# Linear attention and eight routed experts on one core: the overflow spread in two passes, the tails of two experts' q as one block, and the fallback's branch inside the program

## The chip, the cores and the metric

The kernel runs on one core of a Trainium2 chip: TensorE (PE in the tables), VectorE (DVE), ScalarE (ACT), GpSimd (POOL), SyncE (SP) and 16 DMA engines. The metric is the device time of one execution in microseconds, the median of several runs.

## The reference

Attention is linear: q is softmaxed over its 64 head elements, k over the 576 positions of a batch, and each of the 8 heads of a batch has one 64 x 64 matrix kv. Every one of the 4608 tokens (8 batches of 576) then goes to one of eight experts, which is chosen by its id alone; w1 of an expert is 512 x 1024, w2 1024 x 512.

```python
def _attn_ref(q, k, v) -> np.ndarray:
    q_s = q - np.max(q, axis=-1, keepdims=True)
    q_s = np.exp(q_s)
    q_s = q_s / (np.sum(q_s, axis=-1, keepdims=True) + 1e-09)
    ...
    k_s = k_s / (np.sum(k_s, axis=2, keepdims=True) + 1e-09)
    kv = np.einsum('bhsd,bhse->bhde', k_s, v)
    return np.einsum('bhsd,bhde->bhse', q_s, kv).astype(np.float32)
...
    expert_idx = token_ids * np.int64(2654435761) % np.int64(E)
    out = np.zeros((N, D), dtype=np.float32)
    for e in range(E):
        mask = expert_idx == e
        ...
        xe = x[mask]
        h = np.maximum(xe @ w1[e], 0.0)
        out[mask] = h @ w2[e]
```

## The kernel before

**Slots.** Each expert has 640 slots (CAP): 72 for each of the 8 batches (576, MAINC) and 64 for overflow, tokens beyond 72 of one batch and expert. q is gathered by token straight into slot order, five gathers for an expert (four of 128 rows, and a *tail* of 64). Overflow tokens are gathered apart, in batch order, and their X is *spread* to the experts' last 64 slots by matmuls with one-hot matrices.

**Steps.** All work behind the index search is cut into named steps, each a few instructions. The list ORDER, written into the file, is the order in which they are issued; every engine runs its own instructions in that order, and only semaphores tie the engines to each other. SWAP names the evacuations that change between ACT and DVE. A name with `*n` puts n dummy matmuls of 512 columns (line 345) ahead of the step. The names that the text uses:

- K, V: load of a batch's k and v; EK, MK: its exponential and column of ones on ACT; KV: its 20 matmuls; SC: its scaling on DVE (lines 381 to 387), after which kv of the batch can be used.
- G, EQ, SM, ML: gather of a block of q, its exponential, sums over the heads for two or three blocks, scaling; TP, TC: transposition of a block and its evacuation; with an O, the same for overflow.
- CNT, OVA, OHA, FND, FDD: the search for overflow tokens; QS: the one-hots of the spread; ROP, ROD: the row indices of the outputs. CNT also sets a flag that says that some expert has more overflow than its slots hold.
- PP, PC: attention product of blocks of q with the kv of some batches (72 columns for a batch and expert) and its evacuation: this is X, transposed.
- XP, XC: overflow X of two batches, and its copy `xov`; SH, SD: spread of all four, for 128 of the 512 elements, and its evacuation into `XTov`; OV: copy from there into an expert's X.
- W: a half of w1 or w2 of an expert (cast to f16 by the DMA); A: first matmul of an expert (MLP) for a range of slots; R: its relu; B: second matmul of a block of 128 slots; C: its evacuation; S: the scatter of its rows to the output.

**Queues.** k of batches 0 to 2 is loaded by SP; all other loads, gathers and scatters are issued by POOL one after the other, each with a semaphore that it shares with the one eight issues earlier.

**The fallback.** If the flag is set, the scatters write nothing, and `_any_routing` computes everything again in a slower way. Before, the register load of the flag and the branch stand behind all other work (lines 961 to 963); the body is never entered for these inputs.

## Time and profile before

| | |
|---|---|
| median of 3 runs | 224.19 us (224.01 to 224.94) |
| the profiled execution | 224.46 us |
| its span | 222.6 us |
| PE busy | 189.1 us (85%) |
| DVE, ACT, POOL busy | 62%, 52%, 55% |
| DMA queue of POOL | 46.66 MB, 82.0% of the 16 engines' span |

The profile is of one execution. A busy PE is not a PE at its peak: its matmuls overlap, so distances from start to start tell more than durations. "Idle before" names what ended the idle time of an engine. The page's slices are fortieths of the span, 5.57 us each.

### The profile page before, as it was taken

What the parts mean: (1) busy time and instruction counts of PE and PEld (TensorE: products, weight loads), DVE (VectorE), ACT (ScalarE), POOL (GpSimd) and SP (SyncE); (2) the same over time, 40 slices, a digit from 0 to 9 for tenths busy, and PEclk for the clock granted to TensorE, in tenths of its full rate; (3) what the DMA queues carried; (4) which work ended last, traced back from release to release, by engine and by line L of the source; (5) the groups of instructions that cost most, each with busy time, mean ns of one, the idle gap of its engine ahead of it and who ended that gap; (6) DMA issues with size and microseconds to landing.
All of it is one profiled execution on the core that took longest, in us unless ns stands there. A gap on an engine that the chain in (4) does not pass through costs nothing.

```text
span 222.6 us, 3981 instructions
## 1 busy us (share of the span) xinstructions
PE 189.1 (85%) x1533; PEld 124.1 (56%) x1533; DVE 137.8 (62%) x259; ACT 116.6 (52%) x189; POOL 122.9 (55%) x160
## 2 busy tenths in 40 slices
PE   3506165398999999999999999999999999999990
PEld 2507164276567666755776565666665556655540
DVE  6998797668778897697842989675424431022230
ACT  8347555994779877574564655433451224432210
POOL 7675567445378885587785161611543367315661
PEclk9999857559999999999999999999999999999998
DMA  6999999999999999799999968670997999943442
GB/s 209 321 329 389 234 345 329 322 245 296 292 280 274 292 247 267 221 244 233 266 308 216 239 146 155 148 165 3 175 234 167 188 186 195 284 110 135 166 165 85
DMA packets 13543, 50.67 MB, mean 228 GB/s; under 512 B 2650, under 2 KB 2650, under 8 KB 12496
## 3 DMA queue, kind: packets, MB, share of 16 engines
q0 software_dynamic: 12944, 46.66, 82.0%
q1 hardware_dynamic: 576, 3.71, 4.3%
q8 instruction: 13, 0.21, 0.4%
q14 instruction: 10, 0.08, 0.1%
HBM read 63.10 MB, written 10.49 MB: 331 GB/s over the span
## 4 chain that ended last, share of the span: by engine, by line
issue 38%; POOL 21%; PE 20%; DMA 11%; DVE 6%; ACT 2%; POOLq 1%; DVEq 0%
POOL out_dram L550 12%; PE ph L523 7%; DMA kraw<-in_k_dram 4%; PE po L545 4%; DMA out_dram<-ob,sidx 3%; DMA w1r<-in_moe_w_dram 3%; POOL raw L395 3%; PE t L372 2%; POOL w1r L508 2%; PE t L436 2%; PE t L476 2%; POOL w2r L508 2%; DVE A L126 1%; PE t L447 1%; PE t L469 1%
## 5 line engine op out<-in xcount | busy, mean ns | idle before, releaser
L545 PE MATMUL po<-w2r,hT 128*128 128x512 f16 (+2 forms) x328 | 74.8, 374 | 0.0
L523 PE MATMUL ph<-XT,w1r 128*128 128x320 f16 (+2 forms) x512 | 74.6, 297 | 0.0
L536 ACT ACTIVATE hT<-ph 128x640 f16<-128x640 f32 (+3 forms) x58 | 40.5, 703 | 55.3 <-PE ph L523 54.6
L550 POOL DMA_INDIRECT out_dram<-ob,sidx x40 | 42.6, 1065 | 44.7 <-DVE ob L938 29.6
L523 PEld LDWEIGHTS <-w1r 128*128 128x128 f16 x544 | 49.3, 98 | 21.2
L395 POOL DMA_INDIRECT raw<-in_q_dram,gidx x40 | 42.9, 1071 | 20.7 <-issue 4.9
L938 DVE TENSOR_SCALAR ob<-po 128x512 f32<-128x512 f32 x34 | 23.1, 683 | 43.8 <-PE po L545 39.4
L545 PEld LDWEIGHTS <-hT 128*128 128x128 f16 x328 | 30.9, 98 | 30.4
L418 DVE TENSOR_REDUCE rq<-qs 128x16 f32<-128x1024 f16 (+1 forms) x18 | 26.1, 1450 | 3.8 <-ACT qs L406 3.7
L424 DVE TENSOR_TENSOR qs<-qs,rq 128x1024 f16<-128x1024 f16 (+1 forms) x18 | 26.1, 1456 | 0.4
L406 ACT ACTIVATE qs<-raw 128x512 f16<-128x512 f32 (+1 forms) x40 | 23.6, 625 | 0.8 <-DMA raw<-in_q_dram,gidx 0.8
L436 PE MATMUL t<-ident,qs 128*128 128x128 f16 (+1 forms) x176 | 15.8, 226 | 4.8 <-ACT qT L879 2.6
L879 DVE COPY qT<-t 128x512 f16<-128x512 f16 (+3 forms) x18 | 8.5, 478 | 15.6 <-PE t L436 15.3
L508 POOL DMA_DIRECT2D w2r<-in_moe_w_dram x16 | 9.5, 595 | 14.3 <-PE po L545 10.1
L436 PEld LDWEIGHTS <-qs 128*128 128x128 f16 (+1 forms) x176 | 12.0, 103 | 9.1 <-issue 4.3
L372 PE MATMUL t<-v,w1r 128*128 128x129 f16 x64 | 8.0, 293 | 7.5 <-ACT v L360 7.5
L508 POOL DMA_DIRECT2D w1r<-in_moe_w_dram x16 | 9.5, 595 | 5.8 <-PE ph L523 3.7
L372 PEld LDWEIGHTS <-w1r 128*128 128x128 f16 x64 | 6.9, 139 | 7.5 <-issue 7.4
L372 PE MATMUL t<-v,w2r 128*128 128x129 f16 x64 | 5.9, 243 | 5.9 <-DVE rec L381 5.9
L907 DVE CAST XT<-t 128x288 f16<-128x288 f32 (+2 forms) x18 | 7.9, 453 | 4.2 <-PE t L447 3.9
L913 ACT CAST XT<-px 128x864 f16<-128x864 f32 (+1 forms) x7 | 5.6, 811 | 8.6 <-PE px L459 8.6
L879 ACT COPY qT<-t 128x512 f16<-128x512 f16 (+2 forms) x14 | 7.9, 581 | 3.9 <-PE t L436 3.9
(125 smaller groups left out, 187.9 us busy)
## 6 DMA issues: line engine op xcount, KB each, us to landing
w1r<-in_moe_w_dram POOLq DMA_DIRECT2D x16, 512.0 KB, 8.0
w2r<-in_moe_w_dram POOLq DMA_DIRECT2D x16, 512.0 KB, 7.7
kraw<-in_k_dram POOLq DMA_DIRECT2D x3, 1024.0 KB, 9.2
v<-in_v_dram POOLq DMA_DIRECT2D x4, 650.0 KB, 10.2
kraw<-in_k_dram SPq DMA_DIRECT2D x2, 1280.0 KB, 11.2
kraw<-in_k_dram POOLq DMA_DIRECT2D x2, 1280.0 KB
v<-in_v_dram POOLq DMA_DIRECT2D x4, 520.0 KB, 8.5
kraw<-in_k_dram SPq DMA_DIRECT2D x1, 1024.0 KB, 11.3
```

The source lines that it names most:

```text
L372: nc.tensor.matmul(pkv[:, r // 2, r % 2, 0:129], lhsT=k16t[:, f] if last else k16[:, c, f], rhs=v16s[e][:, c * NPAIR + r, 0:129] if last e ...
L395: nc.gpsimd.indirect_dma_start(out=raw[0:w, :], out_offset=None, in_=self.q[:, :], in_offset=bass.IndirectOffsetOnAxis(ap=idx[0:w, i:i + 1 ...
L406: self.nc.scalar.activation(q16[0:w, i].rearrange("p h d -> p (h d)"), raws[i][0:w, :], ACT.Exp)
L418: nc.vector.reduce_sum(rv, qv, axis=AX.X)
L424: nc.vector.tensor_tensor(out=qf, in0=qf, in1=rv.rearrange("p i h -> p (i h)").unsqueeze(2) .to_broadcast([w, (hi - lo) * H_, DH_]), op=AL ...
L436: nc.tensor.transpose(pv[:, r, o:o + w[j]], q16[0:w[j], j, 2 * r:2 * r + 2, :] .rearrange("p h d -> p (h d)"), self.ident[0:w[j], 0:w[j]])
L508: self.nc.gpsimd.dma_start(w[what - 1][:, 2048 * i:2048 * i + 2048], src[e, :, 2048 * i:2048 * i + 2048])
L523: nc.tensor.matmul(p, lhsT=w1r[:, dc, f[i] * 128:(f[i] + 1) * 128], rhs=X[:, dc, :], start=(dc == 0), stop=(dc == DC - 1))
L536: self.nc.scalar.activation(to, fro, ACT.Relu)
L545: nc.tensor.matmul(po[:, 0:d.stop - d.start], lhsT=hT[:, fc, blk * 128:(blk + 1) * 128], rhs=w2r[:, fc, d], start=(fc == 0), stop=(fc == F ...
L550: sc = self.nc.gpsimd.indirect_dma_start(out=self.out[:, :], out_offset=bass.IndirectOffsetOnAxis(ap=self.ix.sidx[:, e, blk:blk + 1], axis=0),
L938: nc.vector.tensor_scalar(out=obs[e, blk][:, d], in0=po[e, blk, x][:, 0:d.stop - d.start], scalar1=1.0 / SX, scalar2=None, op0=ALU.mult)
```

## The change

**Spread in two passes.** SH now multiplies only batches 0 to 3 (the first two `xov`) and SD puts the result into `XTov`. New steps SI and SE do the other half: SE (`join`) adds the bank to what `XTov` holds, in place, on DVE.

**Tails as one block.** Block 4 of an even expert holds its own 64 tail rows and, in partitions 64 to 127, those of the next expert. Odd experts have four blocks. All gathers, exponentials, sums and transposes are of 128 rows, and the transposed tail block is evacuated for both experts at once. Its indices take one matmul more and one DVE operation; the two ACT copies that filled the unused halves go.

**The branch.** A step ANY, behind FDD, loads the flag and jumps over the body, on every engine, while the rest of the program stands behind it. `_any_routing` is rewritten to work with 128 tokens at a time in buffers that the main program has not filled yet; it is never entered here.

**ORDER and SWAP** are other lists. 24 dummy matmuls stand in it (KV2\*9, TPO_1\*7, XP0\*4, PP0_02\*4) where there were 8.

```diff
+        tail = pp[:, NB:NB + E_MOE]
+        nc.tensor.matmul(tail, lhsT=shift[:, 64:192], rhs=g16[:, PLACE[B_ - 1], :], start=True, stop=True)
...
+        V.tensor_scalar(out=gidx[64:128, 0:E_MOE:2, BPE - 1], in0=tail[64:128, 1:E_MOE:2],
+                        scalar1=float(S_ * (B_ - 1) - 1), scalar2=None, op0=ALU.add)
...
-        for i in range(2):
-            nc.scalar.copy(self.q16s[i][64:128, BPE - 1].rearrange("p h d -> p (h d)"),
-                           self.two[64:128, 0:1].to_broadcast([64, D_MOE]))
...
-    def gather(self, idx, widths, lo, hi, into=None):
+    def gather(self, idx, lo, hi, into=None):
         nc = self.nc
         raws = {}
-        for i, w in list(enumerate(widths))[lo:hi]:
+        for i in range(lo, hi):
             raw = into[i] if into else self.qpool.tile([128, D_MOE], F32, tag="qraw", bufs=10)
             nc.gpsimd.indirect_dma_start(
-                out=raw[0:w, :], out_offset=None, in_=self.q[:, :],
-                in_offset=bass.IndirectOffsetOnAxis(ap=idx[0:w, i:i + 1], axis=0),
+                out=raw[:, :], out_offset=None, in_=self.q[:, :],
+                in_offset=bass.IndirectOffsetOnAxis(ap=idx[:, i:i + 1], axis=0),
                 bounds_check=N_TOK - 1, oob_is_err=False)
...
         return pt
 
-    def shared(self, xovs, Qs, r):
+    def shared(self, xovs, Qs, r, ns):
         pr = self.bank("T")
-        for n in range(NBP):
+        for n in ns:
             self.nc.tensor.matmul(pr[:], lhsT=xovs[n][:, r * 128:(r + 1) * 128], rhs=Qs[n],
-                                  start=(n == 0), stop=(n == NBP - 1))
+                                  start=(n == ns[0]), stop=(n == ns[-1]))
         return pr
 
     def spread(self, pr, r):
         put = self.nc.scalar.copy if other(f"SD{r}", r % 2 == 1) else self.nc.vector.tensor_copy
         put(self.XTov[:, :, r, :], pr[:].rearrange("p (e i) -> p e i", e=E_MOE))
+
+    def join(self, pr, r):
+
+        x = self.XTov[:, :, r, :]
+        self.nc.vector.tensor_tensor(out=x, in0=pr[:].rearrange("p (e i) -> p e i", e=E_MOE), in1=x, op=ALU.add)
 
 
 def other(name, put):
...
-def _any_routing(nc, tc, q, k, v, token_ids, w1, w2, out):
+def _any_routing(nc, tc, q, k, v, token_ids, w1, w2, room, ident, w, ps, pool, out):
...
-MK0 EK1 MK1 CNT G0_2 EK0 G0_0 EQ0_2 OVA ZO1 KV1 G0_1 EQ0_0 KV0 EQ0_1 ZO0 OHA FND K3 FDD G0_3 V2 EK2 QS SM0a
...
+ZO0 CNT MK0 OVA G0_2 OHA FND G0_1 G0_0 EK1 V2 ZO1 MK1 EQ0_0 G0_3 EK0 EQ0_2 EQ0_1 K3 EK2 FDD ANY V3 KV1 G0_4
...
-        QW = [128] * (BPE - 1) + [MAINC - 128 * (BPE - 1)]
+
+        def blocks(e):
+            return NBP if e == "O" else BPE - e % 2
         eng = mybir.EngineType
...
+            wts[0] = moe.new_weights(wa)
+
+            def anyway():
+                more = nc.values_load(flag[0:1, 0:1], min_val=0, max_val=1)
+                with tc.If(more > 0, label="any"):
+                    _any_routing(nc, tc, q, k, v, moe_token_ids, moe_w1, moe_w2, (qT, XTs[0], hs[0], at.XTov),
+                                 at.ident, wts[0], ps, fpool, out)
+
+            add("ANY", anyway)
...
+                n = blocks(e)
                 for i in range(n):
                     add(f"G{e}_{i}", gather, e, i, i + 1)
                     add(f"EQ{e}_{i}", lambda e, i: at.expq(qs[e], i, i + 1), e, i)
-                for x, lo, hi in (("a", 0, 2), ("b", 2, 4)) if e == "O" else (("a", 0, 3), ("b", 3, 5)):
...
-                        (A if other(f"TC{e}_{i}", e < 2) else V)(qT[:, :, e % 4, 128 * i:128 * i + sum(QW[i:i + m])], pq[e, i])
-                for i, m in [(i, 1) for i in range(n)] if e == "O" or e < 4 else ((0, 2), (2, 1), (3, 2)):
+                        if i < BPE - 1:
+                            to, fro = qT[:, :, e % 4, 128 * i:128 * (i + m)], pq[e, i]
+                        else:
+                            to, fro = qT[:, :, e % 4:e % 4 + 2, 128 * i:], pq[e, i].rearrange("p r (k t) -> p r k t", k=2)
+                        (A if other(f"TC{e}_{i}", e < 2) else V)(to, fro)
+                for i, m in [(i, 1) for i in range(n)] if e == "O" or e < 4 else ((0, 2), (2, 2), (4, 1))[0:n - 2]:
                     add(f"TP{e}_{i}", lambda e, i, m: pq.update({(e, i): at.turn(qs[e], i, m)}), e, i, m)
                     add(f"TC{e}_{i}", turnc, e, i, m)
             for n in range(NBP):
...
-                add(f"SH{i}", lambda i: pr.update({i: at.shared(xovs, Qs, i)}), i)
+                add(f"SH{i}", lambda i: pr.update({i: at.shared(xovs, Qs, i, (0, 1))}), i)
                 add(f"SD{i}", lambda i: at.spread(pr[i], i), i)
+                add(f"SI{i}", lambda i: pr.update({i: at.shared(xovs, Qs, i, (2, 3))}), i)
+                add(f"SE{i}", lambda i: at.join(pr[i], i), i)
...
-    more = nc.values_load(flag[0:1, 0:1], min_val=0, max_val=1)
-    with tc.If(more > 0, label="any"):
-        _any_routing(nc, tc, q, k, v, moe_token_ids, moe_w1, moe_w2, out)
 
```

On POOL, from the load of k of batch 6 (`kraw_620`, after: `kraw_918`) on, before:

```order
L781 DMA kraw_620<-in_k_dram 128x2560
L785 DMA v_6_625<-in_v_dram 128x2600
L395 DMA raw<-in_q_dram,gidx 128x512
L508 DMA w1r<-in_moe_w_dram 128x2048 x2
L781 DMA kraw_763<-in_k_dram 128x2048
L785 DMA v_7_783<-in_v_dram 128x2080
```

and after:

```order
L785 DMA kraw_918<-in_k_dram 128x2560
L789 DMA v_6_926<-in_v_dram 128x2600
L785 DMA kraw_929<-in_k_dram 128x2048
L789 DMA v_7_933<-in_v_dram 128x2080
L509 DMA w1r<-in_moe_w_dram 128x2048 x2
L396 DMA raw<-in_q_dram,gidx 128x512 x6
```

The two halves of w1 of expert 0 have moved from before k and v of batch 7 to behind them.

On DVE, behind the one-hots of the overflow search (`AO`), before:

```order
L240 TENSOR_TENSOR AO<-rowi,Z 128x2304
L262 COPY ov<-po 64x8 x2
L264 TENSOR_SCALAR of<-ov 128x4
L265 TENSOR_TENSOR of<-ov,obase 128x4
L266 TENSOR_TENSOR oidx<-of 128x4
L268 CAST part<-ov 128x4
L269 CAST part<-obase 128x4
L276 TENSOR_SCALAR Q<-rowi,ov 128x512 x4
L418 TENSOR_REDUCE rq<-qs_109 128x24
```

and after (the body of the branch, which is not entered, stands between the jump and the sums):

```order
L825 MEMSET rawo_292 128x512
L825 MEMSET rawo_293 128x512
L266 COPY ov<-po 64x8 x2
L268 TENSOR_SCALAR of<-ov 128x4
L269 TENSOR_TENSOR of<-ov,obase 128x4
L270 TENSOR_TENSOR oidx<-of 128x4
L272 CAST part<-ov 128x4
L273 CAST part<-obase 128x4
L836 TENSOR_LOAD flag
L837 COMPARE_AND_BRANCH
```

Two memsets and the branch stand in this stretch now; the one-hots `Q` come later.

On PE, the last steps ahead of the first MLP matmul (`ph<-XT`), before: the end of overflow X of batches 4 and 5 (`kvr_106` is batch 5) and a transposition:

```order
L469 LDWEIGHTS qTo_284
L469 MATMUL t<-kvr_106,qTo_284 128x128
L436 LDWEIGHTS qs_109
L436 MATMUL t<-ident,qs_109 128x128
...
L523 LDWEIGHTS w1r
L523 MATMUL ph<-XT_294,w1r 128x432
```

and after: the end of the second spread pass (`xov`, batches 4 to 7), products of expert 1 with batches 6 and 7 (`kvr_107`, `kvr_108`) and with 0 to 3:

```order
L472 LDWEIGHTS xov_1200
L472 MATMUL t<-Q,xov_1200 128x512
...
L443 LDWEIGHTS kvr_107
L443 MATMUL t<-qT,kvr_107 128x72
L443 LDWEIGHTS kvr_108
L443 MATMUL t<-qT,kvr_108 128x72
...
L524 LDWEIGHTS w1r
L524 MATMUL ph<-XT_294,w1r 128x432
```

KV7, the whole first pass of the spread and half of the second, the transposes of expert 1 and most of its products have moved ahead of that matmul.

## Rows read from the trace of the kernel before

**Rows 1.** The page's slices of 5.57 us: TensorE's busy tenths, and its granted clock
```profile
PE   3506165398999999999999999999999999999990
...
PEclk9999857559999999999999999999999999999998
```

**Rows 2.** Timeline of PE: start us, us, engine, line, operation, xcount, idle before
```profile
54.03 0.29 PE L447 MATMUL t<-qT,kvr 128*128 128x72 f16 x4
54.16 0.39 PE L372 MATMUL t<-v,w2r 128*128 128x129 f16 x4
...
56.24 3.08 PE L523 MATMUL ph<-XT,w1r 128*128 128x432 f16 x16
...
60.95 0.39 PE L436 MATMUL t<-ident,qs 128*128 128x128 f16 x4
61.17 0.39 PE L372 MATMUL t<-v,w2r 128*128 128x129 f16 x4
...
62.31 1.62 PE L523 MATMUL ph<-XT,w1r 128*128 128x432 f16 x8
...
63.77 0.61 PE L469 MATMUL t<-kvr,qTo 128*128 128x128 f16 x8
...
64.84 0.44 PE L447 MATMUL t<-qT,kvr 128*128 128x72 f16 x4 [0.33 <-DVE XT L907]
...
65.12 3.62 PE L476 MATMUL t<-Q,xov 128*128 128x512 f16 x16
...
209.54 7.09 PE L545 MATMUL po<-w2r,hT 128*128 128x512 f16 x40
```

**Rows 3.** Timeline of POOL, 49 to 61 us: issues, and the landing waited for
```profile
49.79 1.00 POOL L395 DMA_INDIRECT raw<-in_q_dram,gidx  x1 [1.38 <-DMA v<-in_v_dram]
...
52.62 1.00 POOL L395 DMA_INDIRECT raw<-in_q_dram,gidx  x1 [0.52 <-DMA w1r<-in_moe_w_dram]
...
55.15 0.57 POOL L508 DMA_DIRECT2D w2r<-in_moe_w_dram  x1 [1.53 <-DMA w1r<-in_moe_w_dram]
...
57.56 0.96 POOL L395 DMA_INDIRECT raw<-in_q_dram,gidx  x1 [1.84 <-DMA kraw<-in_k_dram]
...
60.20 1.01 POOL L395 DMA_INDIRECT raw<-in_q_dram,gidx  x1 [1.68 <-DMA v<-in_v_dram]
```

**Rows 4.** Timeline of VectorE (DVE), 24 to 70 us
```profile
24.12 1.14 DVE L276 TENSOR_SCALAR Q<-rowi,ov 128x512 f16<-128x512 f16 x4
...
25.18 1.75 DVE L418 TENSOR_REDUCE rq<-qs 128x24 f32<-128x1536 f16 x1
...
30.15 1.76 DVE L424 TENSOR_TENSOR qs<-qs,rq 128x1536 f16<-128x1536 f16 x1
...
31.82 1.21 DVE L418 TENSOR_REDUCE rq<-qs 128x16 f32<-128x1024 f16 x1
...
33.57 1.22 DVE L424 TENSOR_TENSOR qs<-qs,rq 128x1024 f16<-128x1024 f16 x1
...
39.18 0.16 DVE L381 TENSOR_SCALAR rec<-t 128x4 f32<-128x4 f32 x1
...
40.48 0.29 DVE L879 COPY qT<-t 128x256 f16<-128x256 f16 x1
...
69.08 0.68 DVE L482 CAST XTov<-t 128x512 f16<-128x512 f32 x1
```

**Rows 5.** Lines 961 and 962, the branch: queue, operation, ns, first and last start us
```profile
L961 DVEq TENSOR_LOAD <-flag x1: 541/541/541, 214.9 to 214.9; - x1
...
L962 SPq EVENT_SEMAPHORE  x8: 17/17/17, 14.4 to 18.8; - x8
...
L962 SPq COMPARE_BRANCH  x1: 45/45/45, 14.0 to 14.0; - x1
...
L962 DVEq EVENT_SEMAPHORE  x1: 21/21/21, 216.2 to 216.2; - x1
```

**Rows 6.** Timeline of ACT (ScalarE): a wait at 18 us, a copy of overflow X
```profile
18.18 0.22 ACT L360 COPY v<-two 128x32 f16<-128x32 f16 x1 [2.20 <-DMA v<-in_v_dram]
...
64.42 0.59 ACT L886 CAST xov<-t 128x512 f16<-128x512 f32 x1 [0.64 <-PE t L469]
```

More of the change, by code (lines that the diff above doesn't have):

```diff
@@ L402, in expq @@
     def expq(self, rq16, lo, hi):
-        raws, q16, widths = rq16
+        raws, q16 = rq16
         for i in range(lo, hi):
-            w = widths[i]
-            self.nc.scalar.activation(q16[0:w, i].rearrange("p h d -> p (h d)"), raws[i][0:w, :], ACT.Exp)
+            self.nc.scalar.activation(q16[:, i].rearrange("p h d -> p (h d)"), raws[i][:, :], ACT.Exp)
     def soften(self, rq16, lo, hi):
@@ L429, in turn @@
         nc = self.nc
-        q16, w = rq16[1], rq16[2]
         pq = self.bank("Q")
         pv = pq[:].bitcast(F16).rearrange("p (r t) -> p r t", r=NPAIR)
-        for j in range(i, i + n):
-            o = 128 * (j - i)
+        for j in range(n):
             for r in range(NPAIR):
-                nc.tensor.transpose(pv[:, r, o:o + w[j]], q16[0:w[j], j, 2 * r:2 * r + 2, :]
-                                    .rearrange("p h d -> p (h d)"), self.ident[0:w[j], 0:w[j]])
-        return pv[:, :, 0:sum(w[i:i + n])]
+                nc.tensor.transpose(pv[:, r, 128 * j:128 * j + 128], rq16[1][:, i + j, 2 * r:2 * r + 2, :]
+                                    .rearrange("p h d -> p (h d)"), self.ident[:])
+        return pv[:, :, 0:128 * n]
     def product(self, qT, r, lo, hi, es, q0=0):
@@ L651, in _any_routing @@
                 for dc in range(DC):
                     nc.tensor.transpose(px[:, dc, :], xm[:, dc * 128:(dc + 1) * 128], ident[:])
-                xT = pool.tile([128, DC, 128], F16)
-                nc.scalar.copy(xT[:], px[:])
+                nc.scalar.copy(xT, px)
                 ph = ps.tile([128, 2, 512], F32, tag="S")
@@ L659, in _any_routing @@
                                          start=(dc == 0), stop=(dc == DC - 1))
-                h16 = pool.tile([128, 2, 512], F16)
-                nc.scalar.activation(h16[:], ph[:], ACT.Relu)
-                pt = ps.tile([128, FC, 128], F16, tag="T")
+                nc.scalar.activation(h16, ph[:].rearrange("p i f -> p (i f)"), ACT.Relu)
+                pt = ps.tile([128, 512], F32, tag="Q", name="gq")[:].bitcast(F16).rearrange("p (f t) -> p f t", f=FC)
                 for fc in range(FC):
-                    nc.tensor.transpose(pt[:, fc, :], h16[:, fc // 4, 128 * (fc % 4):128 * (fc % 4) + 128], ident[:])
-                hT = pool.tile([128, FC, 128], F16)
-                nc.scalar.copy(hT[:], pt[:])
-                po = ps.tile([128, D_MOE], F32, tag="O")
+                    nc.tensor.transpose(pt[:, fc, :], h16[:, 128 * fc:128 * fc + 128], ident[:])
+                nc.scalar.copy(hT, pt)
+                po = ps.tile([128, 512], F32, tag="T")
                 for fc in range(FC):
                     nc.tensor.matmul(po[:], lhsT=hT[:, fc, :], rhs=w2r[:, fc, :], start=(fc == 0), stop=(fc == FC - 1))
-                a = acc[:, bass.ds(m, 1), :].rearrange("p o f -> p (o f)")
-                nc.vector.scalar_tensor_tensor(out=a, in0=po[:], scalar=1.0 / SX, in1=a, op0=ALU.mult, op1=ALU.add)
-        nc.sync.dma_start(out.rearrange("(n p c) f -> p n c f", n=NBP, c=C9),
-                            acc[:].rearrange("p (n c) f -> p n c f", c=C9))
+                nc.vector.scalar_tensor_tensor(out=acc, in0=po[:], scalar=1.0 / SX, in1=acc, op0=ALU.mult, op1=ALU.add)
+            nc.sync.dma_start(rows(out)[bass.ds(n, 1), :, bass.ds(c * D_MOE, D_MOE)].rearrange("o p f -> (o p) f"), acc)
 PARTS = ((0, slice(0, 1), ((0, 4), (4, 6), (6, 8))), (1, slice(1, 2), ((0, 4), (4, 8))),
@@ new lines @@
+TPO_3 EK7 SC5 MK7 SH0 SC4 TCO_3 G2_1 PC1_03 KV6 G2_2 TPO_2 SC6 TCO_2 PP0_41 SD3 KV7 SD0 PC0_41 PP0_43 PP0_42
+SC7 XP2 PC0_42 PP0_40 PC0_43 PC0_40 PP1_01 XP3 PC1_01 PP0_61 XC2 G3_0 PP0_62 G3_2 PC0_61 PP1_43 XC3 PC0_62
+W11_1 PP1_40 PC1_43 SI1 PC1_40 SI3 PP1_42 PP1_00 SE1 G3_3 PC1_42 PC1_00 A0_0_2 SI0 EQ3_1 SE3 PP0_63 A0_0_0
+W11_0 PP0_60 G2_3 R0_0_2 SE0 W02_1 SI2 PC0_63 PP1_41 EQ3_0 R0_0_0 W02_0 G5_2 EQ2_1 G4_4 SM3a A0_0_1 R0_0_1
+PC0_60 SE2 A0_0_3 PC1_41 ML3a R0_0_3 A0_576_0 EQ2_2 A0_432_0 A0_432_1 TP3_1 OV1 EQ2_0 R0_432_0 A1_0_0 R0_432_1
@@ L864 @@
             for e in (*range(E_MOE), "O"):
-                n = NBP if e == "O" else BPE
+                n = blocks(e)
                 for i in range(n):
```

269 lines of the change are left out of this document (133 added, 136 removed).

## Prediction

> **What bounds the kernel now.** Read the page's slices first [rows 1]: TensorE (PE) is ragged in the first eleven slices, then at nine tenths or more up to the last; its granted clock is at the lower level (1.2 GHz) in slices 5, 7 and 8 and at 2.4 GHz from slice 9 on. Then the timeline of PE [rows 2]: the first matmul of expert 0's MLP starts at 56.24 us, the last group of matmuls ends at 209.54 + 7.09 = 216.63: 160.4 us in which the slices show no visible hole. The time is therefore one sum: *the moment when the first MLP matmul may start* (call it T), plus the PE work that is still to do then, plus the last scatter and closing barrier. The span is 222.6 us and the profiled execution took 224.46, 0.27 above the median of 224.19; I sum against 224.46 and take the difference over to the median.
>
> What holds T is read from the DMA queue on POOL [rows 3]: POOL's next gather waits again and again for a landing: v of batch 6 by 49.8, the two halves of w1 of expert 0 by 52.6 and 55.15, k of batch 7 by 57.6, v of batch 7 by 60.2. Each is about 1.05 MB read from HBM and each takes 2.4 to 2.8 us: a full pipe in which order is all.
>
> **The change, part by part.**
>
> *The new order at PE.* Before, the first MLP matmul stands behind batches 0 to 6 only; KV7, the spread and expert 1's transposes run after it. Now the first MLP matmul stands behind all of these. What has moved ahead of T, by start-to-start times [rows 2]: KV7, 62.31 - 61.17 = 1.1; the last overflow X, at most 0.6, taken as 0.45; four transposed blocks of expert 1 at 61.17 - 60.95 = 0.22 each, 0.9; eight groups' worth of four 72-column products at 54.16 - 54.03 = 0.13 each, 1.0; 12 of the 16 spread matmuls, 12/16 of 3.62, taken as 2.6 to 2.7. Sum 6.1. The merged tails take another 0.2 off what is left (an estimate: of the transposes behind T, 28 of 64 columns become 12 of 128, these at 0.22/4 = 0.055 each, the short ones at about half). Behind T the old order also waited some 0.65 us around the spread, 0.33 of it in the row at 64.84 and the rest in smaller gaps beside it; that wait would now lie before T. So the new kernel ends when the old one does if T = 56.24 + 6.3 + 0.65 = **63.2 us**; every microsecond of T above or below that is one of the time.
>
> *How early can T be: the loads.* The order list shows w1 of expert 0 ahead of k and v of batch 7 before, and behind them now. V7 moves up by the two halves of w1 (55.15 - 49.79 = 5.4 us), and is pushed back by more q rows ahead of it: nine full gathers of 128 x 512 f32 against four full and two half ones, 1.05 MB, one piece as above, 2.4 us. V7 lands at 60.2 - 5.4 + 2.4 = 57.2, and the second half of w1 at 57.2 + 2 x 2.5 = 62.2. T is not before **62.2**.
>
> *How early: VectorE (DVE).* From its first softmax sum up to the scaling of batch 7, DVE must now do: one three-block sum and scale (1.75 + some 0.6, and 1.76), five two-block sums (33.57 - 31.82 = 1.75), five two-block scales (1.22), eight kv scalings (40.48 - 39.18 = 1.30), the four one-hots of Q (1.14), the four small operations that make row indices (0.9), and nine evacuations of 0.3 to 0.7 (two spread banks like the 0.68 one) [rows 4], 4.3: 4.1 + 8.75 + 6.1 + 10.4 + 1.1 + 0.9 + 4.3 = **35.7 us** without a gap. It can begin at about 24.2: the two memsets ahead of the counts (1 us) only trade places with two behind, so the search for overflow ends 1.4 us earlier than before, at some 22.7, and the branch lies behind it. ACT (ScalarE) needs until 24 for the three exponentials, since its wait for v of batch 1 (18.18, [rows 6]) stays. One gap is certain (the second sum waits for its fifth block of q, which lands near 31: three pieces of 0.4 to 1.05 MB behind k of batch 3, by the same pace): 0.9 us. So batch 7 is scaled at 60.8, and then come the last overflow X 0.45, its copy on ACT 0.59 [rows 6], two of the second-pass spread matmul pairs 0.9 and four hand-offs of 0.15 to 0.25: T = **63.4 to 64.0**. The loads would allow 62.2; DVE is later by 1.2 to 1.8.
>
> *The branch.* It costs each engine a register load and a jump in mid-stream: on DVE 214.9 to 216.2, 1.3 us [rows 5]; the same order on PE, ACT and POOL. On DVE it is covered by the wait for ACT's exponentials; on POOL the queue has several microseconds of transfers outstanding; on ACT it is in front of work that waits for its loads anyway; PE waits there for softmax. Behind the branch on DVE the sum of expert 0 is queued, for which the transposes wait. I take 0, and 1.3 if the covers fail. At the kernel's end its removal is worth nothing: the register load there runs while the last scatter is being issued, and the end waits for that scatter's landing.
>
> *What is off the path.* Four gathers fewer on POOL (1.0 us each, [rows 3]), four exponentials of a half-empty block fewer on ACT, about 4 us of sums and scales less on DVE (four times the difference between a three-block and a two-block sum and scale, 0.6 + 0.5), against four joins of the second pass (one operation over a bank each; the nearest row is the spread's evacuation, 0.68, and I bound a join by half and twice of it). Most of it lies behind T, where PE is the only full engine; the joins of the first two banks stand beside expert 0's first matmuls, and need be done only before the 64-column part. 0 for all of it. The two ACT fills of tails that go stand where ACT next waits for its first data. The extra tail matmul and index operation of expert pairs add 0.2 us ahead of the first gathers; the memset's place covers it. The body of the rewritten branch never runs here.
>
> Sum: T is 63.4 to 64.0 against 63.2, 0.2 to 0.8 us longer; I take 0.6: 225.1 for the profiled run, **224.8** for the median. That is no change that can be measured (0.5% is 1.1 us, about what a measurement can tell).
>
> **The rivals.**
>
> *Slower, by the clock.* In the old run PE was thin between 34 and 44 us and its granted clock was at the lower level up to slice 8 [rows 1]; it rose only near 50 us, when PE had become denser. In the new order PE waits for DVE between KV7 (from 57.5) and T, with some 2 us of work in 5. If the clock falls there, the first matmuls of the MLP run at half speed: the 16 of the first two chunks take 3.08 us at the full one ([rows 2]), so 1.5 to 3 us are lost. For it: the engine was no thinner before its earlier fall. Against: 24 dummy matmuls instead of 8 are put into the waits, though all of them well ahead of KV7. It decides where the clock is low at T: 226.3 to 227.8. Chance 0.2.
>
> *Slower, by front engines that slip.* DVE would be 97% busy for 36 us, in program order. Each wait of DVE for PE's banks adds itself to T. Two more microseconds give 226.8. A dearer branch belongs here: SP jumps at 14.0 us, in a full pipe, and its first semaphore operation follows within half a microsecond [rows 5], so I keep the chance small. But an engine whose next instructions had to be fetched first would stand still, and the fetch would stand behind one to three of the pieces of rows 3 that are in flight, 2.5 to 7.5 us on DVE, which has no slack: 227 to 232. (The Trainium skill, "Runtime: NRT & Kernel Launch", Instruction fetch mechanics, states such a rule: a taken branch whose target is not in the two pages held forces a DMA fetch of that page. By that rule the price above applies where DVE's target lies further on; SP's row shows no such stall, and no run here shows where DVE's target lies.) Chance of a slip 0.17, of the fetch 0.05.
>
> *Faster.* If DVE keeps up and the loads alone bound T (62.2 to 62.5), the time is 223.3 to 223.6. For it: the loads' order is the better one for batch 7. Against: w1 is then needed the moment it lands. More than 0.5% needs T below 62.1, at the bound of the loads, which I know to about 1 us: chance 0.18.
>
> *The halves do not spread.* If both passes ran back to back at the old place the split would only add the joins; the order shows the first pass between batch products, so this is not the case.
>
> **How the numbers follow.** No measurable change 0.40 (own range 223.6 to 225.3); clock 0.2, slip 0.17, fetch 0.05, together slower 0.42; faster 0.18. The range 222.9 to 227.7 leaves out the fetch and about half of the extremes on either side.
>
> **What would show it.** First MLP matmul at 63 to 64 us; V7 landed near 57 and w1 near 62; DVE without a gap from 24 to 60; PE full for 153.4 us (160.4 less 6.3 and 0.65) from T to its last matmul; granted clock at 2.4 GHz when T comes. Wrong would be: T above 65 (slip, or a gap of 3 us behind the branch on DVE or PE), T right but the first 432-column matmuls 364 ns apart (clock), or T near 62 with DVE waiting for loads (faster).

## The result and the profile after

| | before | after |
|---|---|---|
| median of 5 runs each, us | 224.31 (224.01 to 224.94) | 222.05 (221.51 to 222.19) |
| profiled execution | 224.46 | 222.19 |
| first MLP matmul (T) | 56.24 | 62.59 |
| T to the end of the last matmul | 160.4 | 152.5 |
| of it beyond matmuls at their usual distance | 2.0 | 0.3 |
| end of the last matmul to the end of the span | 5.97 | 5.31 |
| outside the span | 1.86 | 1.80 |

The ratio is 0.9888 with an interval of 0.9866 to 0.991: the changed kernel is 1.1% faster. That lies under the predicted range, on the side that was given 0.18. The "usual distance" is from one matmul's start to the next: 0.216 us for 512 columns, 0.182 for 432, 0.136 for 320, 0.056 for 128, 0.029 for 64. Summed over all matmuls from T to the last they make 158.15 us before and 151.93 after.

The slices that answer to [rows 1]. TensorE is still thin in front, but in this execution its granted clock is at 2.4 GHz from 32.1 us to the last matmul. (The nines ahead of that are no sign of the clock: the 129-column products of batch 1, at 27 us, stand 0.11 us apart, those of batch 3, at 35 us, 0.056.)
```profile
PE   3501098669899999999999999999999999999990
...
PEclk9999999999999999999999999999999999999999
```
The timeline of PE that answers to [rows 2]: the second spread pass, the last products ahead of T, T itself, and the last group of matmuls.
```profile
61.47 1.03 PE L472 MATMUL t<-Q,xov 128*128 128x512 f16 x4
...
62.34 0.42 PE L443 MATMUL t<-qT,kvr 128*128 128x72 f16 x8
...
62.59 1.63 PE L524 MATMUL ph<-XT,w1r 128*128 128x432 f16 x8
...
207.99 7.09 PE L546 MATMUL po<-w2r,hT 128*128 128x512 f16 x40
```
The timeline of POOL that answers to [rows 3]. Batch 7 lands before w1 now: v of batch 7 by 57.05 us, the last half of w1 by 62.01.
```profile
52.13 1.00 POOL L396 DMA_INDIRECT raw<-in_q_dram,gidx  x1 [0.52 <-DMA v<-in_v_dram]
54.56 1.00 POOL L396 DMA_INDIRECT raw<-in_q_dram,gidx  x1 [1.43 <-DMA kraw<-in_k_dram]
57.05 1.00 POOL L396 DMA_INDIRECT raw<-in_q_dram,gidx  x1 [1.48 <-DMA v<-in_v_dram]
...
62.01 1.03 POOL L396 DMA_INDIRECT raw<-in_q_dram,gidx  x1 [1.60 <-DMA w1r<-in_moe_w_dram]
```
The timeline of VectorE that answers to [rows 4]: its first sum, its three waits of over a fifth of a microsecond up to the scaling of batch 7, and that scaling, whose last piece ends at 60.07.
```profile
24.74 1.75 DVE L416 TENSOR_REDUCE rq<-qs 128x24 f32<-128x1536 f16 x1 [1.82 <-ACT qs L406]
...
29.48 0.16 DVE L382 TENSOR_SCALAR rec<-t 128x4 f32<-128x4 f32 x1 [0.65 <-PE t L373]
...
47.86 0.42 DVE L895 COPY qT<-t 128x512 f16<-128x512 f16 x1 [0.47 <-PE t L432]
...
59.21 0.86 DVE L388 TENSOR_TENSOR kvr<-t,rec 64x256 f16<-64x256 f32 x2
```
The branch, line 837, that answers to [rows 5] (queue, operation, ns, start us; the last row is a wait of another engine for this line). No engine takes more than 0.6 us from its jump to the semaphore operation behind it, but ACT, whose operation stands behind exponentials that are still running: it comes at 27.1. PE, which has passed at 22.3, waits for it with its products of batch 1, 5.4 us in all.
```profile
L837 ACTq COMPARE_BRANCH  x1: 68/68/68, 21.3 to 21.3; - x1
...
L837 PEldq EVENT_SEMAPHORE  x1: 51/51/51, 22.3 to 22.3; - x1
L837 DVEq COMPARE_BRANCH  x1: 84/84/84, 23.2 to 23.2; - x1
L837 DVEq EVENT_SEMAPHORE  x1: 21/21/21, 23.8 to 23.8; - x1
L837 ACTq EVENT_SEMAPHORE  x1: 17/17/17, 27.1 to 27.1; - x1
...
  PE t L373: 5.4, 1
```
So the time moved in three places: T is 6.35 us later, the stretch from T is 7.9 shorter, and the end is 0.7 shorter: 6.35 - 7.9 - 0.7 = -2.25. The prediction had +7.6, -6.95 and 0.

### The profile page after: what moved, and what is told of

It is laid out like the page before. It is cut to its first block, busy times and chain, and to the rows that moved or that the text cites. A ratio compares the mean times of both kernels' runs of the same rounds, so it can differ in the third digit from the quotient of the medians.

```text
span 220.4 us, 3988 instructions
## 1 busy us (share of the span) xinstructions
PE 187.3 (85%) x1534; PEld 122.3 (55%) x1534; DVE 133.9 (61%) x260; ACT 113.7 (52%) x183; POOL 120.0 (54%) x156
## 4 chain that ended last, share of the span: by engine, by line
PE 51%; DVE 13%; issue 11%; POOL 6%; DMA 4%; POOLq 1%; ACT 1%; ACTq 0%
PE ph L524 24%; PE po L546 19%; POOL out_dram L551 6%; DMA w1r<-in_moe_w_dram 4%; DVE kvr L388 3%; PE t L432 3%; DVE rq L416 3%; DVE qs L422 2%; PE px L455 2%; PE t L443 1%; PE t L373 1%; PE t L472 1%; DVE XT L925 1%; DVE rec L384 1%; DVE Q L280 1%
## 5 line engine op out<-in xcount | busy, mean ns | idle before, releaser
L524 PEld LDWEIGHTS <-w1r 128*128 128x128 f16 x544 | 49.1, 98 | 22.0 <-DMA w1r<-in_moe_w_dram 0.6
L956 DVE TENSOR_SCALAR ob<-po 128x512 f32<-128x512 f32 x32 | 21.6, 682 | 42.3 <-PE po L546 40.4
L416 DVE TENSOR_REDUCE rq<-qs 128x16 f32<-128x1024 f16 (+1 forms) x18 | 23.9, 1328 | 3.3 <-ACT qs L406 3.1
L406 ACT ACTIVATE qs<-raw 128x512 f16<-128x512 f32 x36 | 21.9, 631 | 6.0 <-DMA raw<-in_q_dram,gidx 4.8
L422 DVE TENSOR_TENSOR qs<-qs,rq 128x1024 f16<-128x1024 f16 (+1 forms) x18 | 24.0, 1337 | 0.2
L895 DVE COPY qT<-t 128x512 f16<-128x512 f16 (+1 forms) x19 | 10.0, 528 | 13.7 <-PE t L432 13.7
L432 PE MATMUL t<-ident,qs 128*128 128x128 f16 x160 | 13.7, 222 | 2.9 <-ACT qs L406 2.3
L432 PEld LDWEIGHTS <-qs 128*128 128x128 f16 x160 | 11.1, 100 | 5.2 <-ACT qs L406 2.4
L954 ACT ACTIVATE ob<-po 128x512 f32<-128x512 f32 (+2 forms) x9 | 4.9, 552 | 11.7 <-PE po L546 11.6
L925 ACT CAST XT<-t 128x288 f16<-128x288 f32 (+2 forms) x17 | 6.5, 401 | 8.2 <-PE t L443 8.0
L443 PE MATMUL t<-qT,kvr 128*128 128x72 f16 (+1 forms) x96 | 8.5, 206 | 0.9 <-DVE XT L925 0.7
```

Of the source, the lines that this page charges most:

```text
L406: self.nc.scalar.activation(q16[:, i].rearrange("p h d -> p (h d)"), raws[i][:, :], ACT.Exp)
L416: nc.vector.reduce_sum(rv, qv, axis=AX.X)
L422: nc.vector.tensor_tensor(out=qf, in0=qf, in1=rv.rearrange("p i h -> p (i h)").unsqueeze(2) .to_broadcast([128, (hi - lo) * H_, DH_]), op= ...
L432: nc.tensor.transpose(pv[:, r, 128 * j:128 * j + 128], rq16[1][:, i + j, 2 * r:2 * r + 2, :] .rearrange("p h d -> p (h d)"), self.ident[:])
L524: nc.tensor.matmul(p, lhsT=w1r[:, dc, f[i] * 128:(f[i] + 1) * 128], rhs=X[:, dc, :], start=(dc == 0), stop=(dc == DC - 1))
L925: (A if other(f"PC{e}_{lo}{r}", r % 2 == 0) else V)(X[:, es, r, lo * CELL:hi * CELL], px[e, r, lo])
```

## Experiments

Each run is timed against the kernel before on the same chip; ratios are to that, and the changed kernel's own is 0.9888. "T", "gaps" (what lies between T and the last matmul beyond the usual distances) and "tail" (end of the last matmul to the end of the span) are read from the profiled execution of each. Medians of different rows are not all from the same chip, so the ratios are what to compare, and two whose intervals overlap are not told apart by the time.

| run | median us | ratio (95%) | T | gaps | tail |
|---|---|---|---|---|---|
| kernel before | 224.3 to 224.8 | 1 | 56.24 | 2.02 | 5.97 |
| changed kernel | 222.05 | 0.9888 (0.9866 to 0.991) | 62.59 | 0.33 | 5.31 |
| b_tail128 | 223.91 | 0.9975 (0.995 to 1.0) | 55.25 | 0.76 | 6.52 |
| b_noend | 223.53 | 0.9951 (0.9929 to 0.9974) | 56.26 | 2.02 | 4.80 |
| b_both | 222.66 | 0.9927 (0.9901 to 0.9953) | 55.37 | 0.75 | 4.79 |
| b_spin | 223.98 | 0.9973 (0.9943 to 1.0002) | 54.77 | 2.92 | 5.86 |
| a_nofall | 221.30 | 0.986 (0.9837 to 0.9882) | 61.84 | 0.41 | 4.79 |
| a_endany | 222.57 | 0.9915 (0.9882 to 0.9948) | 62.04 | 0.62 | 6.41 |
| a_early | 221.87 | 0.9878 (0.9857 to 0.99) | 62.46 | 0.20 | 5.32 |
| a_nohint | 222.08 | 0.9904 (0.9879 to 0.9929) | 62.49 | under 0.1 | 5.31 |
| a_dve | 223.70 | 0.9968 (0.9937 to 0.9999) | 63.50 | 0.92 | 5.32 |
| a_best | 221.68 | 0.9875 (0.984 to 0.991) | 62.78 | 0.22 | 4.97 |
| a_qs | 221.90 | 0.9904 (0.9877 to 0.993) | 62.08 | 0.34 | 5.32 |
| a_onepass | 224.39 | 0.9991 (0.9967 to 1.0015) | 62.94 | 0.58 | 5.31 |
| a_nospin | 223.61 | 0.9985 (0.9956 to 1.0015) | 62.88 | 0.32 | 6.48 |
| a_thin | 223.45 | 0.9927 (0.9897 to 0.9957) | 63.93 | 0.82 | 5.31 |

**What a half-width tail costs.** In the kernel before, seven half tails are transposed behind T. One of them on PE's timeline; "64*128" is the part of the array that is used:
```profile
81.79 1.11 PE L523 MATMUL ph<-XT,w1r 128*128 128x320 f16 x7
82.84 0.29 PE L436 MATMUL t<-ident,qs 64*128 64x64 f16 x4
83.06 0.72 PE L523 MATMUL ph<-XT,w1r 128*128 128x320 f16 x4
```
From 82.84 to 83.06 are 0.22 us for four matmuls of 64 columns, which at 0.029 make 0.12: 0.09 too much behind them, and 0.10 ahead (the matmul before starts at 82.60 and should be followed after 0.136). Run b_tail128 is the kernel before with

```diff
-                nc.tensor.transpose(pv[:, r, o:o + w[j]], q16[0:w[j], j, 2 * r:2 * r + 2, :]
-                                    .rearrange("p h d -> p (h d)"), self.ident[0:w[j], 0:w[j]])
+                nc.tensor.transpose(pv[:, r, o:o + 128], q16[:, j, 2 * r:2 * r + 2, :]
+                                    .rearrange("p h d -> p (h d)"), self.ident[:])
```

> The kernel before, with the transposes of the half-empty tail blocks done over all 128 partitions and 128 columns (the unused half holds finite numbers that no later step reads); gathers, exponentials, sums and evacuations stay as they are. The two traces show PE gaps of 0.10 us ahead of and 0.09 us behind each of the seven half tails that are transposed behind the first MLP matmul before, and no such gap after. Theory N (the switch to 64 partitions and back is what costs): the seven pairs of gaps, 1.3 us, vanish, 28 transposes are each 0.027 us longer (0.75), so 0.5 to 0.6 us less than before: ratio 0.997 to 0.998, and no gap beside a tail in the trace. Theory P (the prediction: a tail costs its columns and nothing else; the gaps belong to a wait for a bank or an evacuation): the gaps stay, 0.7 us more: ratio 1.003.

The same place in that run:
```profile
79.82 2.20 PE L523 MATMUL ph<-XT,w1r 128*128 128x320 f16 x15
81.86 0.39 PE L436 MATMUL t<-ident,qs 128*128 128x128 f16 x4
82.08 1.25 PE L523 MATMUL ph<-XT,w1r 128*128 128x320 f16 x8
```
Four matmuls of twice the columns take the same 0.22 us from start to start. All 14 gaps are gone; the gaps fall from 2.02 to 0.76 us while the matmuls grow by 0.76. The edit changes rows and columns at once, but columns are not the cause: in the kernel before, 32 matmuls of 64 columns over all 128 rows stand among wider ones, without a gap. They start 8 x 0.056 us after the group ahead of them, and the next group follows after 32 x 0.029:
```profile
69.57 0.61 PE L436 MATMUL t<-ident,qs 128*128 128x128 f16 x8
70.02 1.10 PE L523 MATMUL ph<-XTov,w1r 128*128 128x64 f16 x32
70.95 0.39 PE L436 MATMUL t<-ident,qs 128*128 128x128 f16 x4
```
So it is shown that the turn to 64 rows and back is what costs: 7 x 0.19 = 1.3 us that the merged tails take away. The ratio is the one that theory N gave, and theory P's 1.003 lies outside its interval, but the fit is partly luck: in this execution T came 1.0 us earlier too, on which b_spin, below, bears, and the last scatter landed 4.2 us after its issue instead of 3.7, which makes the tail 0.55 longer.

**The branch, at the end and in the middle.** b_noend is the kernel before without lines 961 to 963 and without the prefetch hint for the branch, a_endany the changed kernel with these lines and the old body of the fallback put back and ANY taken out of ORDER, a_nofall the changed kernel with neither.

> The kernel before without the branch at its end and without the fallback behind it (left out, as is the prefetch hint for it; the flag is still computed). Theory P (the prediction): nothing, since the end waits for the last scatter: ratio 1.000. Theory N (from the two traces: from the last matmul to the end of the span 5.97 us before and 5.32 us after): 0.6 us less, ratio 0.997, and the last scatter's landing and the closing waits some 0.6 us nearer to its issue.

> The changed kernel without the branch in its middle and without the fallback (left out, with the hint). In the trace of the changed kernel PE's products of batch 1 wait until 27.12 us for ACT to pass the branch, and VectorE waits 0.65 us for them at 29.48. Theory P (VectorE's chain sets the first MLP matmul, T): the products start near 24.1, VectorE's wait goes, T falls from 62.6 by 0.5 to 0.7 us and the time with it: ratio to before 0.986. Theory L (the landing of w1 at some 61.9 us and the PE work queued behind it set T): T stays within 0.2 us and the ratio is 0.988 to 0.989, as of the changed kernel.

> The changed kernel with the branch back at the end, behind all other work, with the fallback of the kernel before; the rest as changed. The run without any branch had T (first MLP matmul) at 61.84 us and 6.9 us from its last matmul to the end of the execution; the kernel before, with its branch at the end, has 7.8 there, and instruction packets of 16 and 8 KB at 217.7 to 218.7 us between the issue and the landing of its last scatter. Theory E (a branch costs wherever it stands: 0.75 us of T in the middle, about 1 us of landing at the end): T 61.8, gaps as of the changed kernel, last scatter's issue to the end of the span 5.4 to 5.9 us, ratio to before 0.989 to 0.991, the same as or up to 0.5 us slower than the changed kernel. Theory P (prediction: the end branch is free): ratio 0.986, as without any branch.

The end is read in the DMA view of the stretch from the last scatter's issue on: instruction packets by their queues, and the last line is the scatter with its time to landing in us. Before (217.2 to 221.5 us):
```profile
q8 instruction: 1, 0.02, 2.2%
q14 instruction: 2, 0.02, 1.7%
issues: line engine op xcount, KB each, median us to landing
out_dram<-ob,sidx POOLq DMA_INDIRECT x1, 3.7
```
and in b_noend (217.2 to 221 us), where no instruction packet is left in the stretch:
```profile
q0 software_dynamic: 160, 0.44, 30.4%
issues: line engine op xcount, KB each, median us to landing
out_dram<-ob,sidx POOLq DMA_INDIRECT x1, 2.6
```
After it is 2.6 as well; in a_endany three instruction packets are back and it is 4.1. Theory E holds: a_endany's interval leaves out theory P's 0.986. With the branch at the end instruction packets are fetched just then, and the last scatter lands 1.1 to 1.5 us later after its issue. The same goes for all runs: it lands after 3.6 to 4.2 us in the five with a 16 KB instruction packet between issue and landing (before, b_tail128, b_spin, a_endany, a_nospin), and after 2.6 us in the ten others whose landing is in the trace. Part of it is lost again behind the landing: tail and the time outside the span together are 7.8 us before, 8.2 in a_endany, 7.1 after, 7.0 and 6.9 without a fallback.

In the middle the branch costs T: 62.59 with it, 62.04 and 61.84 without. Without it, in a_nofall, PE's products of batch 1 follow the overflow search at once; with it they wait for ACT. The first row is of the changed kernel, the second of a_nofall:
```profile
27.12 0.59 PE L373 MATMUL t<-v,w1r 128*128 128x129 f16 x4 [5.38 <-ACTq L837]
21.50 0.59 PE L373 MATMUL t<-v,w1r 128*128 128x129 f16 x4
```
(The expectation was 24.1.) By the traces, then, moving the branch gained 0.7 us at the end against the kernel before, or 1.1 against a_endany, and gave back 0.55 to 0.75: between nothing and half a microsecond net. The ratios of a_endany and of the changed kernel, 0.9915 and 0.9888, are too close to show it. The prediction had 0 for either.

> The changed kernel with the branch ahead of the exponential of k of batch 2 instead of behind it, so that ACT passes it some 2.5 us earlier. Everything is computed. Both theories: PE's products of batch 1 start near 24.7 us instead of 27.12 and VectorE's wait of 0.65 us for them goes. Theory P (VectorE's chain sets T): T falls by 0.4 to 0.6 us, ratio to before 0.986. Theory L (w1's landing sets T): T within 0.2 us, ratio 0.988 to 0.989.

> The changed kernel without the prefetch hint for the branch (four instructions at the program's start). Theory F (an engine that jumps must fetch the instructions behind the jump, unless they were fetched ahead): VectorE, ACT or PE stands still behind the jump, more than the 0.6 us from the end of the jump to the next instruction in the trace of the changed kernel; T later by 0.5 to 3 us. Theory 0 (the hint does nothing here): T within 0.2 us of 62.6, ratio 0.988 to 0.989.

In a_early ACT passed at 25.0, the products of batch 1 started at 25.07 and VectorE's wait of 0.65 us went, but its first sum, at 25.01, now waited for ACT's passage of the branch, so a quarter microsecond went back at once, and 0.3 us more in waits for the products of batches 4 and 7. T fell by 0.13, which is what theory L gave and less than theory P did: one run that does not speak for VectorE alone. The hint does nothing that shows (T 62.49).

**What sets T.** a_dve puts two memsets of 128 x 512 f32 ahead of SC7.

> The changed kernel with two more memsets on VectorE (128 x 512 f32 into a tile that nothing reads, 0.5 us each) right ahead of the scaling of batch 7. Theory P (VectorE's chain sets T): T goes from 62.6 to 63.6, ratio to before 0.993. Theory L (w1's landing sets T, VectorE has slack): T stays within 0.3 us, ratio 0.989.

VectorE and PE in that run:
```profile
58.70 0.48 DVE L859 MEMSET late<- 128x512 f32 x1
59.35 0.48 DVE L859 MEMSET late<- 128x512 f32 x1 [0.17 <-DVE late L859]
...
60.11 0.86 DVE L388 TENSOR_TENSOR kvr<-t,rec 64x256 f16<-64x256 f32 x2
```
```profile
63.24 0.42 PE L443 MATMUL t<-qT,kvr 128*128 128x72 f16 x8
63.50 0.71 PE L524 MATMUL ph<-XT,w1r 128*128 128x432 f16 x3
```
0.9 us more ahead of the scaling of batch 7, T 0.9 later. VectorE has no slack. (The time rose by more than T: behind T the gaps are 0.6 us longer, nearly all of it one wait for VectorE's evacuation of an output block at 146 us.) To shorten its chain, a_qs moves QS into its wait of 1.8 us ("FDD ANY QS EK2"), and a_best moves the branch further ahead as well ("EQ0_0 ANY FND ... FDD QS ZO1").

> The changed kernel with the branch ahead of the exponential of k of batch 2, and with the one-hots Q (1.2 us on VectorE) moved from behind the scaling of batch 1 to right behind the branch, into the gap in which VectorE waits for ACT's exponentials. Everything is computed. Theory P (VectorE's chain sets T, the loads are next): VectorE gives up 1.2 us between its first sum and the scaling of batch 7, T falls from 62.6 (62.46 with the early branch alone) until w1's landing holds it: 61.9 to 62.2, ratio to before 0.985 to 0.987. Theory L (loads set T already): T 62.4 to 62.6, ratio 0.988.

> The changed kernel with another order in front: the branch ahead of the exponentials of k of batch 0 and of the two last blocks of expert 0 on ACT, and ahead of the overflow search's last matmuls on PE; the one-hots Q and the second pair of memsets behind the search on VectorE, in its gap of 1.8 us ahead of the first sum. Everything is computed. Theory P (VectorE's chain sets T, and ACT's passing the branch is what the products of batch 1 wait for): these products start near 22 us instead of 27.1, VectorE's gaps of 1.82 and 0.65 us shrink to under 0.5 together, T 61.3 to 61.9 (not below the landing of w1), ratio to before 0.984 to 0.986. Theory L (loads alone): T 62.3 to 62.6, ratio 0.988.

a_qs took T to 62.08, as theory P has it, and no further: now VectorE waits 0.2 us each for the products of batches 4 and 7 (those of 7 wait for ACT, which waited 0.4 us for k of batch 7), and w1 has landed by 61.8. In time that is nothing that can be measured. a_best missed: ACT, which jumps at 22.1 now, starts the exponential of batch 0 at 22.62 instead of 21.25, and VectorE's first sum comes at 26.12; what QS and the earlier products (at 22.60, with ACT's passage at 22.5) gave is lost there. Of these 1.4 us 0.5 are ACT's wait at the branch; 0.8 lie ahead of it, where ACT waited longer for the first block of q. VectorE's chain and the loads are within half a microsecond of each other; neither version is told apart from the changed kernel by its time.

**The split.** a_onepass multiplies all four `xov` in SI's place (`at.shared(xovs, Qs, i, (0, 1, 2, 3))`), with SD in SE's.

> The changed kernel with the spread in one pass at the place of the second: all four overflow blocks in one group of matmuls, its evacuation where the join was; the first pass is gone. Eight matmuls of 512 columns move from a stretch where PE waits anyway to the path: four ahead of T and four behind it, 0.86 us each way. VectorE loses two evacuations of 0.69 us ahead of the scaling of batch 7. If VectorE's chain sets T, T changes by 0.86 - 0.7 (one of the two evacuations was on VectorE close ahead of batch 7) = 0.2 to 0.9 and PE behind T has 0.86 more: 1.0 to 1.7 us slower than the changed kernel, ratio 0.993 to 0.997. If the split is worth nothing: 0.989.

T came 0.35 us later and the matmuls behind it grew by 0.87; with 0.25 more of gaps that is 1.4 us in the profiled executions, as expected, and 2.3 between the medians, which is more than expected; what the rest is stays open. The split is worth 1.4 to 2.3 us in this order.

**The dummies, the clock and a packet.** a_nospin is the changed kernel without any `*n`, a_thin with dummies of 64 columns, b_spin the kernel before with TP0_2\*2, TPO_1\*4 and XP1\*9.

> The changed kernel without its 24 dummy matmuls. In the trace of the changed kernel TensorE's granted clock is at 2.4 GHz from 32.1 us on, in the kernel before (8 dummies) at 1.2 GHz from 36.1 to 49.7 us. Theory C (the dummies keep the clock up, and the clock matters): the granted clock is at 1.2 GHz in part of 33 to 50 us, VectorE waits for PE's products of batches 2 to 5, T later by 0.5 to 1.5 us, ratio 0.991 to 0.996. Theory D (VectorE's work alone sets T, PE has slack in front even at 1.2 GHz): T within 0.3 us of 62.6, ratio 0.988 to 0.990. If the clock is still low when T comes: 1.5 to 3 us later, ratio above 0.996.

> The changed kernel with its 24 dummy matmuls 64 columns wide instead of 512, at the same places: the same number of instructions, an eighth of the columns. Without any dummies the clock was low from 41.4 to 51.7 us, T was 62.88, and the tail from the last matmul to the end of the span was 6.48 us instead of 5.31, with a 16 KB instruction packet at 216.45 us between issue and landing of the last scatter. Theory A (two separate things: the columns keep the clock up, the number of instructions sets where instruction packets fall): clock low in part of 36 to 52 us, T 62.6 to 63.0, tail 5.3 us and no 16 KB packet behind the last scatter's issue; ratio 0.989 to 0.991. Theory B (the tail of the run without dummies came from the clock or the shifted work): tail 6 us or more again, ratio 0.994 and above.

> The kernel before with 15 more dummy matmuls of 512 columns: 2 and 4 ahead of the transpositions of expert 0's block 2 and of overflow block 1, 9 ahead of the second overflow X, all in 38 to 44 us where PE is thin. In the kernel before TensorE's clock is at 1.2 GHz from 36.1 to 49.7 us and batches 4 and 5 are multiplied at that clock; in the run with full-width tails it rose at 47.1 and T was 55.25 instead of 56.24. Theory C (the low clock in front sets T of the kernel before): clock up by 45 us, T 54.5 to 55.4, time 0.8 to 1.7 us less, ratio 0.992 to 0.997. Theory D (loads set T; w1 lands at 55.15, and the dummies only fill idle time): T 56.0 to 56.4, ratio 0.999 to 1.002. If the dummies wait for banks and push PE back: T later, ratio above 1.002.

TensorE's granted clock in the slices of 5.5 us, a_nospin first, a_thin second and b_spin third; before it is in [rows 1]:
```profile
PEclk9999999758999999999999999999999999999997
```
```profile
PEclk9999999656999999999999999999999999999999
```
```profile
PEclk9999758699999999999999999999999999999998
```
Without dummies the clock is at 1.2 GHz from 41.4 to 51.7 us, and T is only 0.3 later; the clock was back at 2.4 GHz well ahead of T. So theory D had T, and none had the end, where the larger part of a_nospin's loss is, 1.2 us; a_thin tells why: with the number of instructions restored the tail is back at 5.31, though the clock was low from 40.3 to 53.9 us. In a_nospin an instruction packet falls behind the last scatter's issue, with no branch near (215.9 to 221 us):
```profile
q8 instruction: 1, 0.02, 1.9%
issues: line engine op xcount, KB each, median us to landing
out_dram<-ob,sidx POOLq DMA_INDIRECT x1, 3.8
```
a_thin's T of 63.93 is beyond what theory A gave, and the trace says where it comes from. Its clock rose 2.2 us later than a_nospin's, so the products of batch 5 and the work behind them ran at 1.2 GHz up to 53.9 us, and VectorE waited for the products of batch 4. The scaling of batch 4, in a_nospin first and in a_thin second:
```profile
55.00 0.16 DVE L382 TENSOR_SCALAR rec<-t 128x4 f32<-128x4 f32 x1
55.97 0.16 DVE L382 TENSOR_SCALAR rec<-t 128x4 f32<-128x4 f32 x1 [0.96 <-PE t L373]
```
That wait is nearly all of the 1.05 us between the two T; the loads landed no later. So the low clock in front costs T 0.3 us or 1.3, by when it ends. (This execution was the slowest of a_thin's eight, 223.98; the fastest took 222.39.) In b_spin, the old order with the clock up from 42.3 us, T came 1.5 us earlier, as theory C has it, which also fits b_tail128, where the clock rose 2.6 us earlier than before: what held T of the kernel before was the clock, not its loads. But only 0.6 of it was kept, and the ratio's interval reaches 1: PE then ran into batch 7, whose v lands at 60.2 in that order, and waited 0.57 us, and 0.33 more at 81 us:
```profile
59.48 0.39 PE L436 MATMUL t<-ident,qs 128*128 128x128 f16 x4
60.28 0.39 PE L372 MATMUL t<-v,w2r 128*128 128x129 f16 x4 [0.41 <-ACT v L360]
```

**Do they add?** b_both has the edits of b_tail128 and b_noend together.

> The kernel before with both earlier edits: tails transposed over 128 partitions and columns, and no branch and no fallback (left out). If the two gains add: 0.9975 x 0.9951 = 0.9926; the tails' gaps gone in the trace, 4.8 us from the last matmul to the end of the span. What the run without any branch of the changed kernel has beyond that (ratio 0.986) is then what order, split and the merge's narrower work are worth: 1.5 us. If they don't add (the one hides the other): 0.995 to 0.9975.

They add: 0.9927 against 0.9926. This makes a rough account. Without a fallback, the old order with full-width tails has the ratio 0.9927 and the new one 0.986: 1.5 us, of which 0.9 are the 16 transposes (28 against 12, at 0.056) that b_both's unmerged tails have too many. Some 0.6 us are left for the new order, the split and the dummies together, no more than the intervals allow for noise; the split alone is worth more (a_onepass), so in one pass the new order would be slower than the old. The switches at the tails are 1.3, the branch nothing to 0.5, the merge's fewer columns 0.1. The sum is 2.0 to 2.5, against 2.3 measured.

## Why the prediction was wrong

The frame held: T, the work behind T, and the end. What T does to the last matmul is one to one within 0.1 us in a_nofall, a_qs and a_nospin (in a_dve and a_thin 0.5 to 0.6 more); VectorE sets T, the loads are half a microsecond behind. One reading of the kernel before failed without a price: b_spin shows that its T was held by the clock and not by the loads. Three terms of the sum were mis-sized, all on the same side.

- **"The merged tails take another 0.2 off what is left."** The columns were counted (by the prediction's own figures they give 0.1), the switch of the array to 64 partitions and back was not: 0.19 us at each of seven places, 1.3 us. The rows for it were in the trace of before; what hid them was the step "160.4 us in which the slices show no visible hole". Two microseconds are 1.3% of that stretch, and a digit of a slice can't show it. A sum of matmuls at their usual distance, 158.15, set against 160.17 from T to the last start, would have. The part of it that I did find, 0.65 around the spread, was right. From T to the end PE took 152.5 us where 153.4 were predicted; a new wait of 0.44 at 104 us, for a w1, is in it, without which it would have been some 1.4 less than predicted.
- **"At the kernel's end its removal is worth nothing."** The reason given, that the end waits for the last scatter's landing, is true, and the landing is what the branch delayed: 3.7 us against 2.6. The end came 0.7 us nearer to the last matmul, and b_noend, without branch and fallback, has the ratio 0.9951, whose interval leaves out the predicted 1.000.
- **T = 63.4 to 64.0.** It was 62.59. VectorE's chain was predicted at 35.7 us of work and 0.9 of waits from 24.2, with batch 7 scaled at 60.8; it had 34.2 and 1.1 from 24.7, and was through at 60.07. The eight scalings (10.3), the first sum (4.1), the row indices and Q were right to 0.2; too dear were the evacuations (3.6 against 4.3), the two-block sums (8.4 against 8.75) and scales (5.85 against 6.1). Evacuations and scales were summed by their durations, and a record overlaps the next one's: the scale at 52.30 takes 1.21 us, and the next operation starts after 1.13. From there to T it was 2.5 us; 2.6 to 3.2 were given, though the terms named for it add up to 2.5 to 2.9. v of batch 7 landed by 57.05 and w1 by 62.01, predicted 57.2 and 62.2.

Taken together: T 1.2 us less than the 63.8 that the sum used, 0.9 less behind it, 0.7 less at the end, 2.8 us under the 225.1 of the profiled run, close to what was measured (222.19). The miss in T would have been larger but for a fourth term of the other sign, which hid in it:

**The branch in the middle** was taken at 0 "and 1.3 if the covers fail". It cost T 0.55 to 0.75. The covers for the register load and the jump held, but the step that "PE waits there for softmax" failed: the branch tied the engines. Behind it PE's wait for ACT, whose data for batch 1 had been there since 18.4 us, was met only when ACT itself had passed: at 27.1, 25.0, 24.6 and 22.5 us in the changed kernel, a_early, a_qs and a_best, and the products started within 0.1 us of it each time; without a branch they started at 21.50.

**The rivals.** The clock was up from 32 us on and did not fall ahead of T. In no run was it low at T, so the price that this rival named, the first MLP matmuls at 1.2 GHz, was not put to the test; what a low clock further in front costs is 0.3 us of T in a_nospin and 1.3 in a_thin. The engine that stands still for its instructions did not show in the middle, with or without the hint: four more instruction packets of 8 KB than in a_nofall are in the trace between 18 and 28 us, of 0.3 to 0.4 us each, and no engine but ACT, which is busy, takes more than 0.6 us from its jump to its next operation on semaphores. (The Trainium skill, "Runtime: NRT & Kernel Launch", Instruction fetch mechanics, has a taken branch wait for a fetch of its target where that is not in the two pages held. No row here shows such a wait in the middle; at the end of the kernel before the fetches are in the trace, and what came late there was the scatter's landing.) The rival that won, "faster", was given 0.18 for another reason, T at the bound of the loads; at T = 62.59 and the prediction's break-even of 63.2 that would have been 0.6 us, a quarter of the gain.

## What to carry to other kernels

Where one engine is full for most of the span, add up its instructions at their usual distance and set the sum against the clock time of the stretch: the difference names losses that no slice shows, here 2 us, 1.3 of it at matmuls that use half of the array's rows. Price the program's end by its last landing, and look there for instruction packets. A branch across all engines can also make one engine wait until another has passed it, so its place is to be chosen by the engine that passes it last.

## What the runs showed of the hardware

- A matmul over 64 partitions among matmuls over 128 cost 0.10 us ahead and 0.09 behind, at each of the seven places behind T; full-width ones, with unused rows, cost nothing of the kind. (The Trainium skill, "TensorEngine Tiling (Array Packing)", Key Properties, says that a change of the tiling mode drains TensorE, without a time; the gaps agree.)
- A scatter of 128 rows of 2 KB lands 2.6 us after its issue where no instruction packet is under way, and 3.6 to 4.2 us after it where one to three are (fifteen traces). One was there in all four runs with the branch at the end; of the others only in a_nospin, where 24 matmuls fewer moved one into the last scatter.
- The hint for the branch had no effect that shows, and a jump in mid-stream took SP, PE and VectorE 0.5 to 0.6 us from the jump to the semaphore operation behind it.
- An engine's wait for another engine, behind a branch that both pass, was met within 0.1 us of the other's passage in four traces, and at once, 5.6 us earlier, in the run without the branch.
